# Batch 2's shifted copy of V moved from GpSimd's DMA queue to SyncE's, and batch 3's V preparation moved a few slots later

## The chip, the cores and the metric

The kernel runs on one core of a Trainium2 chip. Its time is the device time of one execution in microseconds (us); a figure for a kernel is the median of several executions. The engines of the core are called PE (TensorE: matrix products; PEld is its weight load), DVE (VectorE), ACT (ScalarE), POOL (GpSimd) and SP (SyncE, which here only issues DMAs). They run beside each other, each in its own order, and wait for one another by semaphores.

## The reference

Sliding-window causal attention (window 64, 8 batches, 8 heads, 576 positions, head size 64), then a layer norm and a two-layer MLP with a residual:

```python
scores = scale * np.matmul(q, k.transpose(0, 1, 3, 2))
mask = (rel >= 0) & (rel < window)          # rel = row position - column position, window = 64
scores = np.where(mask, scores, -1000000000.0)
attn = np.exp(scores - np.max(scores, axis=-1, keepdims=True))
attn = attn / (np.sum(attn, axis=-1, keepdims=True) + 1e-09)
x = np.matmul(attn, v)                      # then heads side by side: (8, 576, 512)
xn = (x - mu) / np.sqrt(var + 1e-06) * g_ln
out = x + np.maximum(xn @ w_ch1, 0.0) @ w_ch2   # 512 -> 2048 -> 512
```

## The kernel before

The first 512 rows of each batch are one group of 4 blocks of 128 rows; the last 64 rows of all 8 batches are a ninth group, "the tails". The main loop runs over groups g. PE's work in iteration g is the MLP of group g, written as a list of **units** (32 at g = 1: 16 units `l1_half` of 8 matmuls each, L586, and 16 units `l2` of 4 matmuls each, L456, four for each block). After unit i the kernel emits what was put into **slot** i with `at(i, function, arguments)`: the attention of batch g + 1 and the loads and casts of batch g + 2. There is no scheduler: within a slot, and so on each engine, the order of the `at` calls is the order of execution.

In iteration g = 1 the work around batch 2 and batch 3 is this.

- **V of batch 2.** `load_v` (L141) brings 512 rows of V in four 256 KB DMAs on SP's queue into `v32`, of which there is one buffer. `cast_v` (L147, POOL) casts it to fp16 into `vA`. The window of a block of 64 query rows reaches into the block of 64 keys before it, so a second copy `vB`, shifted by 64 rows, is made: `alloc_vB` (L151, POOL) clears the first 64 rows, and `make_vB` (L165 and L166) copies `vA` into `vB` with two DMAs from SBUF to SBUF, of 64 partitions each: 260 KB and 195 KB, issued on POOL's queue.
- **The product with V.** `b_pe` (L343, PE) multiplies the masked exponentials `pt` with `vA` and `vB`. Block 0 of batch 2 stands in slot 14, blocks 1, 2 and 3 in slots 17, 20 and 20. Block 0 needs the first of the two copies only. Its PSUM tile `xps` has one buffer, which held the scores of block 1 before; so it also needs ACT's second exponential of these (L309, slot 13).
- **Rows of x.** `b_rows` (L359 to L368, DVE) divides by the sums and takes mean and variance (`mvg`). `z_step` (L387 to L390, POOL) makes the normalized rows `z` of the block in four operations, and `zt_step` (L398) transposes them with a DMA on SP's queue into `zT`. The MLP of group 2 starts with `hps` (L444), whose first matmul needs all four transposes of batch 2. Its PSUM bank (two buffers) is that of block 2's `ch`, its second unit's that of block 3's; they are emptied by `add_out` (L466, DVE).
- **Batch 3.** SP issues its q and k in two halves (L94, slots 3 and 8), then its V (slot 10). POOL casts the first half of q and k in slot 8 (L128), the second in slot 14 behind block 0's `z_step`, and V, in two halves, in slot 18 (ahead of them the last element of each head's row is set to one, L135). `vB` of batch 3 is cleared and made in slot 20.

SP takes its instructions strictly in order, waits included.

Of the kernel before, what the change touches and what calls it, by code (L numbers as in the profile page):

```python
# [20 lines left out]
def kernel(  # L21
# [10 lines left out]
    nc = tc.nc  # L32
# [48 lines left out]
    qkT, vA, vB, pts = {}, {}, {}, {}  # L81
# [79 lines left out]
    def vB_prev(b, c, eng):  # L161
        evac(eng, vB[b][0:64, c + 1, :, 0:D], v32[b][64:128, c])

    def make_vB(b):
        nc.gpsimd.dma_start(out=vB[b][64:128, :], in_=vA[b][0:64, :])  # L165
        nc.gpsimd.dma_start(out=vB[b][0:64, 1:4], in_=vA[b][64:128, 0:3])  # L166

    wst = {}

# [619 lines left out]
    for i in range(8):  # L789
# [7 lines left out]
        out=mask[0:64], in_=mask[0:64], compare_op=ALU.is_gt, fill=0.0,  # L797
# [3 lines left out]
        out=mask[64:128], in_=mask[64:128], compare_op=ALU.is_ge, fill=0.0,  # L801
# [88 lines left out]
    for g in range(NGRP):  # L890
# [7 lines left out]
        def at(i, f, *a):  # L898
            slots[min(i, len(slots) - 1)].append((f, a))

        def first_scores(b, i):
            at(i, s_pe, b, 0)
            at(i, s_pe, b, 1, False, "xps")
            at(i, s_exp, b, 0, 0, 1)
            at(i + 1, s_exp, b, 1, 0, 1)
            at(i + 1, s_mask, b, 0)
            at(i + 2, s_mask, b, 1)

        b = g + 1
# [33 lines left out]
        if g == 1:  # L943
            at(0, cast_qk, 2, 0)
            at(0, cast_qk, 2, 1)
            at(0, b_step, 1, 2)
            at(2, b_step, 1, 3)
            at(4, zt_step, 1, 2)
            at(4, root, 1)
            at(6, zt_step, 1, 3)  # L950
            at(4, alloc_v, 2)
            at(4, alloc_qkT, 2)
            at(4, alloc_vB, 2)
            at(5, cast_v, 2, 0, 4)
            at(5, make_vB, 2)
            at(4, t_main, 2, 0, 0)
            at(5, t_main, 2, 1, 0)
            at(7, t_main, 2, 0, 1)
            at(7, t_main, 2, 1, 1)
            at(7, w2_sums, 3, 0, 4)  # L960
            at(8, w2_sums, 3, 4, 8)
            at(25, w2_sums, 2, 0, 4)
            at(28, w2_sums, 2, 4, 8)
            at(9, s_pe, 2, 0)
            at(9, s_pe, 2, 1, False, "xps")
            at(9, s_exp, 2, 0, 0, 1)
            at(10, s_mask, 2, 0)
            at(11, s_exp, 2, 1, 0)
            at(13, s_exp, 2, 1, 1)
            at(13, s_mask, 2, 1)  # L970
            for j in range(4):
                i = (14, 17, 20, 22)[j]
                if j < 3:
                    at(i, b_pe, 2, j)
                if j < 2:
                    at(i, s_mm, 2, j + 2)
                    at(i + 1, s_mask, 2, j + 2)
                if j == 2:
                    at(i, b_pe, 2, 3, "sc")
                at(i, b_rows, 2, j)  # L980
                at(i, z_step, 2, j)
                at((18, 21, 24, 27)[j], zt_step, 2, j)
            at(3, load_qk, 3, 0)
            at(8, load_qk, 3, 1)
            at(10, load_v, 3, 0, 4)
            at(8, alloc_qkT, 3)
            at(8, cast_qk, 3, 0)
            at(14, cast_qk, 3, 1)
            at(18, alloc_v, 3)
            at(18, cast_v, 3, 0, 2)  # L990
            at(18, cast_v, 3, 2, 4)
            at(20, alloc_vB, 3)
            at(20, make_vB, 3)
            first_scores(3, 30)
            for i, (x, half) in zip((12, 24, 18, 28), ((0, 0), (1, 0), (0, 1), (1, 1))):
                at(i, t_main, 3, x, half, 0)
            at(40, load_qk, 4, 0)
            at(40, load_qk, 4, 1)
            at(40, load_v, 4, 0, 2)
# [58 lines left out]
        if g > 1 and n < B:  # L1058
            at(3, load_v, n, 2, 4)
            at(17, alloc_v, n)  # L1060
            at(17, cast_v, n, 0, 2)
            at(17, cast_v, n, 2, 4)
            at(21, alloc_vB, n)
            at(21, make_vB, n)
            for i, (x, half) in zip((13, 18, 13, 22) if g == 2 else (13, 17, 13, 21),
                                    ((0, 0), (1, 0), (0, 1), (1, 1))):
                at(i, t_main, n, x, half, 0)
            first_scores(n, 27)
            if n + 1 < B:
                at(40, load_qk, n + 1, 0)  # L1070
                at(40, load_qk, n + 1, 1)
                at(40, load_v, n + 1, 0, 2)
# [61 lines left out]
```

## Time and profile before

| | us |
|---|---|
| median of three runs (308.37, 309.27, 311.14) | 309.27 |
| profiled execution | 308.48 |
| span from first to last instruction of the profiled execution | 306.6 |
| PE busy | 293.8 (96%) |
| DVE busy | 215.3 (70%) |
| POOL busy | 172.8 (56%) |
| ACT busy | 150.2 (49%) |
| mean granted clock of TensorE | 0.991 |

The profile's times count from the start of the span. A line of the timeline gives start, duration, engine, line, operation, output<-inputs, how many, and in brackets the idle time of the engine before it with the releaser. A line of the chain of waits gives start, duration and what ran. A line of a table by stages gives the stretch, its length, the busy time of each engine with the number of instructions, the granted clock (1.00 is full), the busy share of the DMA engines (above 1 where transfers overlap) and GB/s. "us to landing" runs from the start of a DMA's issue to its completion. A wait for several things is put down by the profile to the one that came last by its records.

### The profile page before, as it was taken

To read this page: it belongs to the slowest core of one execution; us is meant where nothing else is said; L and a number is where in the kernel's file an instruction comes from. 1 tells how busy PE (TensorE), PEld (TensorE's weight loads), DVE (VectorE), ACT (ScalarE), POOL (GpSimd) and SP (SyncE) were. 2 spreads that over 40 slices of the span, in tenths; PEclk is the share of its full clock that TensorE was granted. 3 is DMA by queue.
4 is the path that set the end of the run, shared out by engine and by line. 5 is a ranking of instruction groups with operands and counts; after the bars stand their busy time and mean duration, and the time that the engine had idled before them with its cause. 6 is when DMAs were issued, how large, how long until landed. Compare 5 with 4: busy or idle time off the path is not lost.

```text
span 306.6 us, 7574 instructions
## 1 busy us (share of the span) xinstructions
PE 293.8 (96%) x3061; PEld 196.7 (64%) x3061; DVE 215.3 (70%) x416; ACT 150.2 (49%) x253; POOL 172.8 (56%) x258
## 2 busy tenths in 40 slices
PE   6999999997998999999999999999999999999992
PEld 4557545785454459755965597559655854788882
DVE  0688695763573898469856874699568875789972
ACT  2496635686216753785247527852475046306500
POOL 7589676472791778378817964688128507014300
PEclk9999999999899999999999999999999999999998
DMA  8999999999756999799269997996619397003014
GB/s 192 265 385 303 314 362 270 282 262 244 156 125 188 285 188 162 219 321 181 41 206 319 191 195 214 318 136 97 214 31 181 69 188 190 19 17 139 0 37 103
DMA packets 113669, 58.35 MB, mean 190 GB/s; under 512 B 83617, under 2 KB 104609, under 8 KB 113634
## 3 DMA queue, kind: packets, MB, share of 16 engines
q1 hardware_dynamic: 112576, 54.67, 73.9%
q0 software_dynamic: 768, 2.80, 3.8%
q8 instruction: 24, 0.39, 0.6%
q10 hardware_dynamic: 290, 0.40, 0.5%
q14 instruction: 11, 0.09, 0.1%
HBM read 38.80 MB, written 9.44 MB: 157 GB/s over the span
## 4 chain that ended last, share of the span: by engine, by line
PE 85%; DMA 4%; ACT 3%; DVE 3%; SPq 3%; POOL 1%; issue 1%; POOLq 0%
PE hps L444 29%; PE pA L521 12%; PE pB L521 8%; PE pC L521 8%; PE ch L456 5%; PE xps L343 4%; PE sc L299 3%; PE hph L586 3%; SPq L141 3%; DMA vB<-vA 2%; PE ch L603 2%; PE tp L229 2%; PE lA L641 2%; PE warm L811 2%; DMA v<-in_v_dram 1%; PE lC L641 1%
## 5 line engine op out<-in xcount | busy, mean ns | idle before, releaser
L444 PE MATMUL hps<-zT,w1g 128*128 128x512 f16 x416 | 94.6, 379 | 0.9 <-DVE xn L466 0.9
L448 ACT ACTIVATE hrT<-hps 128x512 f16<-128x512 f32 x104 | 62.4, 600 | 42.1 <-PE hps L444 38.7
L444 PEld LDWEIGHTS <-w1g 128*128 128x128 f16 x416 | 39.2, 98 | 46.4 <-issue 3.4
L309 ACT ACTIVATE pt<-sc 128x512 f16<-128x512 f32 x72 | 39.3, 599 | 26.2 <-PE sc L299 25.6
L387 POOL TENSOR_SCALAR rsz<-mvg 128x1 f32<-128x1 f32 x28 | 10.9, 390 | 63.5 <-DVE mvg L368 62.5
L521 PEld LDWEIGHTS <-sS 128*128 128x128 f16 x448 | 43.3, 98 | 4.9
L128 POOL CAST qk<-qk 128x1024 f16<-128x1024 f32 x32 | 35.6, 1126 | 11.2 <-DMA qk<-in_k_dram 4.6
L316 DVE TENSOR_TENSOR pt<-pt,mask 128x1024 f16<-128x1024 f16 x32 | 25.3, 795 | 19.5 <-ACT pt L309 19.5
L521 PEld LDWEIGHTS <-hrT 128*128 128x128 f16 x336 | 32.1, 98 | 6.4 <-ACT hrT L448 1.0
L215 ACT COPY qkT<-tp 128x1024 f16<-128x1024 f16 x16 | 16.1, 1013 | 34.0 <-PE tp L229 24.2
L521 PE MATMUL pC<-w2s,sS 128*128 128x256 f16 x224 | 26.9, 273 | 0.0
L521 PE MATMUL pA<-wT,sS 128*128 128x256 f16 x224 | 26.9, 273 | 0.0
L363 DVE TENSOR_TENSOR xn<-xps,rcp 128x512 f32<-128x512 f32 (+1 forms) x47 | 25.6, 564 | 0.9
L365 DVE BATCH_NORM_STATS2 stats<-xn 128x6 f32<-128x512 f32 x36 | 25.0, 695 | 1.2
L495 DVE TENSOR_TENSOR sS<-hrT 128x512 f16<-128x512 f16 (+1 forms) x40 | 24.2, 606 | 2.2 <-ACT hrT L448 2.1
L586 PE MATMUL hph<-zT,w1g 128*128 128x256 f16 x192 | 23.7, 276 | 0.6 <-DVE zT L407 0.5
L390 POOL TENSOR_SCALAR z<-xn,rsz 128x512 f16<-128x512 f32 x28 | 21.9, 782 | 2.9
L359 DVE RECIPROCAL rcp<-xps 128x8 f32<-128x8 f32 (+1 forms) x47 | 7.7, 183 | 19.3 <-PE xps L343 19.3
L388 POOL TENSOR_TENSOR rsz<-rsz,mhalf 128x1 f32<-128x1 f32 x28 | 19.8, 706 | 2.3
L586 PEld LDWEIGHTS <-w1g 128*128 128x128 f16 x192 | 18.2, 99 | 3.4 <-DVE zT L407 0.7
L456 PE MATMUL ch<-w2s,hrT 128*128 128x512 f16 x80 | 20.0, 398 | 0.0
L343 PEld LDWEIGHTS <-pt 128*64 128x64 f16 x576 | 11.5, 110 | 12.6 <-issue 8.0
(116 smaller groups left out, 443.0 us busy)
## 6 DMA issues: line engine op xcount, KB each, us to landing
out_dram<-xn SPq DMA_DIRECT2D x33, 256.0 KB, 2.4
qk<-in_q_dram SPq DMA_DIRECT2D x16, 512.0 KB, 6.5
qk<-in_k_dram SPq DMA_DIRECT2D x16, 512.0 KB, 7.3
v<-in_v_dram SPq DMA_DIRECT2D x32, 256.0 KB, 7.5
w2s<-in_moe_w_ch_dram SPq DMA_DIRECT2D x9, 512.0 KB, 9.3
w1s<-in_moe_w_ch_dram SPq DMA_DIRECT2D x4, 512.0 KB, 6.6
tk<-in_k_dram SPq DMA_DIRECT2D x8, 256.0 KB, 4.7
tv<-in_v_dram SPq DMA_DIRECT2D x8, 256.0 KB, 5.0
```

Of the source, the lines that this page charges most:

```text
L128: nc.gpsimd.tensor_copy(out=dst[:, :].rearrange("p (a j) e d -> p a e j d", j=j), in_=t[:, :].rearrange("p (a e j d) -> p a e j d", e=2, j ...
L309: nc.scalar.activation(out=o, in_=i, func=AF.Exp, bias=0.0, scale=scale)
L316: nc.vector.tensor_tensor(out=ptv, in0=ptv, in1=mb, op=ALU.mult)
L343: nc.tensor.matmul(out=tiles[h // n][64 * r:64 * r + 64, h % n, :D + 1], lhsT=pt[:, par, hp, r, :], rhs=rhs, start=True, stop=True)
L363: nc.vector.tensor_tensor(out=xn[:, n * i:n * i + n], in0=xps[:, :, 0:D], in1=rcp_b, op=ALU.mult)
L365: nc.vector.bn_stats(out=stats, in_=xv)
L444: nc.tensor.matmul(out=hps, lhsT=w1g[:, kc, 128 * hc:128 * (hc + 1)], rhs=zT[g][:, kc, :], start=(kc == 0), stop=(kc == NKC - 1),)
L448: nc.scalar.activation(out=hrT[:, hc, :], in_=hps, func=AF.Relu, bias=0.0, scale=1.0)
L456: nc.tensor.matmul(out=ch[kb], lhsT=hrT[:, hc, 128 * kb:128 * (kb + 1)], rhs=w2s[:, hc, :], start=(hc == 0), stop=(hc == NHC - 1),)
L495: nc.vector.tensor_tensor(out=o, in0=x, in1=y, op=op)
L521: nc.tensor.matmul(out=o, lhsT=a[:, c, 128 * p:128 * p + 128], rhs=wv[:, c, :], start=(first and (p == 0 or split_c) and c == 0), stop=(c ...
L586: nc.tensor.matmul(out=hps[:, e], lhsT=w1g[:, kc, 128 * hc:128 * (hc + 1)], rhs=zT[g][:, kc, 256 * half:256 * half + 256], start=(kc == 0) ...
```

## The change

`make_vB` takes the issuing engine as an argument. Batch 2's copy (g = 1, slot 5) is issued on SP's queue; the one call of `make_vB` with another engine than POOL. On SP's queue slot 5 lies behind the first half of batch 3's q and k (slot 3) and ahead of the second (slot 8) and of batch 3's V (slot 10).

For batch 3 the second half of the V cast goes from slot 18 to 21, and `alloc_vB` and `make_vB` (still on POOL's queue) from slot 20 to 23. On POOL the order after block 1's `z_step` was: cast of both halves, `z_step` of block 2, clearing of `vB`, two DMA issues, `z_step` of block 3. It becomes: cast of the first half, `z_step` of block 2, cast of the second half, `z_step` of block 3, clearing of `vB`, two DMA issues. No other engine's order changes.

```diff
-    def make_vB(b):
-        nc.gpsimd.dma_start(out=vB[b][64:128, :], in_=vA[b][0:64, :])
-        nc.gpsimd.dma_start(out=vB[b][0:64, 1:4], in_=vA[b][64:128, 0:3])
+    def make_vB(b, eng=nc.gpsimd):
+        eng.dma_start(out=vB[b][64:128, :], in_=vA[b][0:64, :])
+        eng.dma_start(out=vB[b][0:64, 1:4], in_=vA[b][64:128, 0:3])
...
             at(5, cast_v, 2, 0, 4)
-            at(5, make_vB, 2)
+            at(5, make_vB, 2, nc.sync)
...
             at(18, cast_v, 3, 0, 2)
-            at(18, cast_v, 3, 2, 4)
-            at(20, alloc_vB, 3)
-            at(20, make_vB, 3)
+            at(21, cast_v, 3, 2, 4)
+            at(23, alloc_vB, 3)
+            at(23, make_vB, 3)
```

## The prediction

> **What bounds the kernel now.** PE is busy for 96% of the span, so a gain must close PE's idle time, give it a better clock, or leave it less to do. I first asked who PE waits for:
>
> ```profile
> PE xps L343 <- DMA vB<-vA: 2.2, 1, 2.2
> PE hps L444 <- DVE xn L466: 0.9, 1, 0.9
> ```
>
> Columns: total us, how often, longest. Apart from a 2.3 us start-up wait these are the two largest waits of PE, both inside iteration g = 1. The first is the transfer that the change moves. The chain of waits shows it in place:
>
> ```profile
> 64.87 1.90 POOL vA L147
> 66.77 0.29 issue
> 67.06 7.63 DMA vB<-vA
> 74.69 0.14 issue
> 74.83 0.45 PE xps L343 x16
> 75.28 0.34 PE sc L299 x16
> 75.62 1.48 PE hph L586 x8
> 77.09 2.91 PE ch L456 x8
> 80.00 0.38 PE xps L343 x16
> ```
>
> The copy of batch 2's V lands 7.63 us after POOL issued it, and block 0's product with V starts at 74.83. What follows is slow too: 8 hph matmuls in 1.48 us, 8 ch matmuls in 2.91. The table by stages says why (busy time of PE, PEld, DVE, ACT and POOL, then the granted clock, the DMA share and GB/s):
>
> ```profile
> 72.60:74.80 2.20, 0.00 (x1) 0.00 (x0) 0.69 (x1) 0.66 (x2) 0.00 (x0) 1.00 1.07 207
> 76.30:77.00 0.70, 0.70 (x5) 0.52 (x4) 0.68 (x1) 0.44 (x1) 0.00 (x0) 0.50 0.40 83
> 77.00:78.00 1.00, 1.00 (x4) 0.34 (x3) 0.76 (x2) 0.60 (x1) 0.54 (x2) 0.50 1.02 228
> 78.00:79.00 1.00, 1.00 (x3) 0.30 (x2) 0.00 (x0) 0.00 (x0) 0.79 (x3) 0.50 0.73 166
> ```
>
> After 2.2 us without a matmul the clock falls to half, to be back only at about 79.2. POOL's timeline and one line of SP's give the other wait its cause:
>
> ```profile
> 77.38 0.44 POOL L387 TENSOR_SCALAR rsz<-mvg 128x1 f32<-128x1 f32 x1 [5.35 <-DVE mvg L368]
> ...
> 79.66 2.02 POOL L128 CAST qk<-qk 128x1024 f16<-128x1024 f32 x2
> 82.40 0.53 POOL L387 TENSOR_SCALAR rsz<-mvg 128x1 f32<-128x1 f32 x1 [0.72 <-DVE mvg L368]
> ...
> 84.80 2.03 POOL L147 CAST vA<-v 128x1024 f16<-128x1024 f32 x2
> 86.92 0.19 POOL L387 TENSOR_SCALAR rsz<-mvg 128x1 f32<-128x1 f32 x1
> ...
> 91.03 0.18 POOL L387 TENSOR_SCALAR rsz<-mvg 128x1 f32<-128x1 f32 x1
> ...
> 92.33 0.76 POOL L390 TENSOR_SCALAR z<-xn,rsz 128x512 f16<-128x512 f32 x1
> ```
>
> ```profile
> 93.11 1.20 SPq L398 DMA_TRANSPOSE zT<-z x1
> ```
>
> PE stops at 95.24 and goes on at 96.10 with hps. The profile names the add L466 that ended at 96.04, but the first hps unit takes the bank of block 2's ch, emptied by 91.45; only the second needs the later one. It also needs all four transposes, and the last of them, of block 3's z (ended 93.09), took 2.7 us from 93.11. So POOL's z chain holds PE here, some 3.0 us from the end of z to the first matmul. From 96 to 301 us PE has no idle time worth naming: 204.86 us busy of 205.00. What g = 1 gains goes to the end.
>
> **Part 1, the copy on SP's queue.** POOL loses two DMA issues (0.75 + 0.53 us, 67.06 to 68.36); it idles 0.89 us right after, until q arrives, so that is worth nothing. SP gains two issues and a wait: the first must wait for the V cast, over at 66.77. Queued behind it are batch 3's second q/k half (issued at 64.05 and 64.60 before), its four V loads (from 66.79) and all transposes.
>
> The trace has no such copy on SP's queue. An SP issue costs 0.33 us (out store) to 1.10 us (the q load at 62.30). From issue to landing: at best 2.3 us (the out store of 256 KB at 96.06, in a quiet queue), at worst 10.6 us (a V load issued at 67.2). So the first copy lands between 66.8 + 2.3 = 69.1 and 77.4. I take about 71.5, because of one row: the q load issued at 64.05 took 8.4 us and landed at 72.45, right behind the k load issued at 63.50 (7.4 us, 70.9). The copy takes that q load's place behind the k load with half its bytes, and no second queue beside it.
>
> Then PE no longer waits for the copy. Next is ACT: block 0's tile is free only when the exponential at 72.18 ends (0.59 us), so it starts at 72.85 instead of 74.83: **1.98 us**. A wait of 0.25 us takes the place of 2.23.
>
> The clock: 8 hph and 8 ch matmuls took 75.62 to 80.00, 4.38 us. At full clock 8 hph take 0.88 (63.80 to 64.68) and 8 ch 1.75 (half of the 3.45 and 3.56 of 16): 2.63. **1.75 us**; the table gives the same: 2.7 us at 0.50, with 0.7 us at 0.75 ahead of them and 1 us at 0.82 behind, lose 1.35 + 0.18 + 0.18 = 1.7. In sum block 1's product starts at 76.3 instead of 80.00: 3.7 us ahead.
>
> The Trainium skill, "TensorE: Matmul & The Clock Gate", section "HAM oscillation", gives as its rule that PE gaps above some 3.4 us are the ones that cost the clock. By it this gap of 2.2 us would be free and the 1.75 us would drop out of the sum; the row shows half clock after it, and decides.
>
> The q/k half issued after the copies starts some 4 us later, at 68.0. Two loads at the distances seen (1.5 and 0.9 us) behind the copies land by about 75. POOL casts them once block 0's z is done, which after the change is 77.9: a cover of 3 us. The V loads start near 69 and land near 80 to 81, as before or 1 us later; the first two are wanted at 82.3, the last two at 86.
>
> **Part 2, and the end of the chain.** PE's ch ends at 95.25 - 3.71 = 91.54. Is z there? Block 0's rows now start behind the mask (72.81, 0.69 us) that stands ahead of them on DVE, so `mvg` comes 1.87 us after 73.5, and POOL starts z at 75.56. From there on POOL has work without a break, by the durations above: z of block 0 2.31 (77.38 to 79.69), two casts 2.02, z of block 1 2.40, the ones and half a V cast 1.1, z of block 2 2.48 (86.92 to 89.40), the other half 1.0, z of block 3 2.06, some 0.15 between. That is 13.5 us: z ends at 89.1 and hps starts 3.0 later, at **92.1**. Without part 2, clearing and issuing (89.35 to 91.03, 1.7 us) would stand ahead of z, and hps would start at 93.8. So PE waits 0.55 us where it waited 0.86, and iteration 2 starts at 92.1 instead of 96.10: **4.0 us** earlier. If it had been the add L466 after all, hps would start at 91.54 + 0.85 = 92.4; the sum hardly depends on it.
>
> Batch 3's `vB` is issued behind z: cleared by 89.6, landed 3.9 us (the 89.82 issue's time) later at 93.5. Its first reader stood 2.7 us behind hps, so at 94.8: 1.3 us to spare. If that cover goes, PE waits there.
>
> The sum: 1.98 + 1.75 + 0.86 - 0.55 = 4.0 us. The profiled execution took 308.48 (span 306.6), so 304.5. That execution lies 0.8 below the median of the three runs; I keep its own time as base, and the range has room for the rest.
>
> **The rivals.**
>
> *The copy comes late, but earlier than before.* The DMA engines were full from 67 to 75 us (busy share above 1), and an empty slot arises while SP waits for the cast. If it lands at 74.0, block 0 starts at 74.1, POOL's chain ends 1.25 us later (hps at 93.35), PE's own way at 92.8 with the full clock or 94.5 with the loss. 305.8 to 306.9. Against it: the 72.45 row.
>
> *It does not do what it says.* If the bytes ahead set the landing and not the queue, the copy lands at 74.7 as ever. Then part 2 alone acts: z is 1.7 us earlier, and the 0.86 us goes. 307.6.
>
> *The other side.* SP's queue is worse than POOL's for this copy: it waits behind everything SP has issued, and transfers issued on SP in those microseconds took 7.1 to 10.6 us. The product starts later than before from 8.0 us on (66.8 + 8.0 = 74.8), and the whole is slower from 8.9, when the 0.86 us is used up too. At 10.6 us block 0 starts at 77.5, 2.7 us late, with the clock lost as before; less the 0.86 us, 1.8 us slower: 310.3. Against it: those 8.4 to 10.6 us were spent behind 1 to 2 MB, of which only some half a megabyte would be left ahead of the copy.
>
> A rule speaks for this rival: "DMA: Bandwidth & Descriptors", section "Queues, rings and completion order", has each DMA engine take turns between queues packet by packet. On a queue of its own the copy should get its turn at once, and giving that up should cost. The measured 7.6 us for 260 KB, against 3.9 at 89.82 in a quieter stretch, shows little of such a privilege.
>
> **How the numbers follow.** Forecast, 303.4 to 305.5 (POOL's durations good to half a us, PE's own way alone giving 303.9): 0.67. Late copy, 305.8 to 306.9: 0.16. No effect of part 1, 307.6: 0.09. Slower, 310.3: 0.08. Predicted 304.5; leaving out the last case and most of what lies above, the range is 303.2 to 307.7. About 1% (3.1 us) is what a measurement of this kernel can tell from no change. Faster by over 1%, below 305.4: 0.66. Slower by over 1%, above 311.6, needs the last case and more: 0.04. Within: 0.30.
>
> **What would show it.** The wait of xps on vB gone from PE's list, block 0's product right behind the exponential of slot 13, half clock nowhere between 72 and 84 us; block 1's product near 76.3; POOL without a break from 75.6 to 89; hps starting 3 us after block 3's z, and half a microsecond of idle PE before it. It would be wrong if the copy took over 6 us, if batch 3's second q/k half landed after 77.9 (each microsecond later moves z and hps as much), or if batch 3's `vB` came after 94.8.

## The result and the profile after

The changed kernel takes 306.07 us (median of six, 305.05 to 307.14) where the kernel before took 310.14 in the same batches (six, 308.37 to 311.38): 4.1 us, a ratio of 0.987 with the 95% interval 0.983 to 0.991. A second measurement gave 0.988 (0.984 to 0.991). Ratios in this document leave disturbed executions out (those over 1.5% above the fastest of their kernel); medians and spreads count all. The profiled execution took 305.05 us, its span 303.2.

PE's waits from 90 us to the end of the span (after), ACT's second exponential of block 1's scores, and the start of block 0's product with V on PE's timeline:

```profile
PE hps L444 <- DMA zT<-z: 1.3, 1, 1.3
```

```profile
71.94 0.59 ACT L309 ACTIVATE pt<-sc 128x512 f16<-128x512 f32 x1
```

```profile
72.63 0.19 PE L343 MATMUL xps<-vB,pt 128*64 128x65 f16 x1 [0.27 <-issue]
...
76.06 0.22 PE L343 MATMUL xps<-vB,pt 128*64 128x65 f16 x1
...
92.64 2.79 PE L444 MATMUL hps<-zT,w1g 128*128 128x512 f16 x12 [1.28 <-DMA zT<-z]
```

The 2.2 us wait for vB is gone, 0.27 us is left; the profile names no releaser for it ("issue"), but ACT's exponential ended at 72.53, 0.1 us before the product, while the copy had landed at 71.4. Block 1's product follows 3.43 us later, where it took 5.17. The wait before hps is now put down to the transpose itself, and has grown from 0.86 to 1.28 us. SP's timeline, and the landing time of its first copy:

```profile
61.70 0.38 SPq L94 DMA_DIRECT2D qk<-in_q_dram  x1
62.17 0.59 SPq L94 DMA_DIRECT2D qk<-in_k_dram  x1
68.08 0.56 SPq L165 DMA_DIRECT2D vB<-vA  x1
68.68 0.58 SPq L166 DMA_DIRECT2D vB<-vA  x1
69.32 0.60 SPq L94 DMA_DIRECT2D qk<-in_q_dram  x1
69.96 0.86 SPq L94 DMA_DIRECT2D qk<-in_k_dram  x1
70.86 6.56 SPq L141 DMA_DIRECT2D v<-in_v_dram  x4
```

```profile
vB<-vA SPq DMA_DIRECT2D x1, 260.0 KB, 3.3
```

SP stands still from 62.8 to 68.08, until POOL has cast batch 2's V (1.3 us later in this execution than in the profile before), and then the copy lands in 3.3 us, at 71.4. The table by stages (busy PE, PEld, DVE, ACT, POOL, then granted clock, DMA share, GB/s) has full clock where it was half:

```profile
72.60:74.80 2.20, 2.17 (x43) 1.75 (x44) 2.13 (x4) 1.77 (x4) 0.00 (x0) 1.00 0.99 301
...
77.00:78.00 1.00, 1.00 (x6) 0.49 (x5) 0.97 (x2) 0.97 (x2) 1.00 (x2) 1.00 1.20 221
78.00:79.00 1.00, 1.00 (x7) 0.44 (x5) 0.97 (x4) 0.00 (x0) 1.00 (x2) 1.00 1.02 208
```

And POOL's chain, from block 0's z to block 3's:

```profile
75.22 0.46 POOL L387 TENSOR_SCALAR rsz<-mvg 128x1 f32<-128x1 f32 x1 [4.29 <-DVE mvg L368]
...
77.49 2.48 POOL L128 CAST qk<-qk 128x1024 f16<-128x1024 f32 x2
...
85.75 1.04 POOL L147 CAST vA<-v 128x1024 f16<-128x1024 f32 x1
...
88.41 0.76 POOL L390 TENSOR_SCALAR z<-xn,rsz 128x512 f16<-128x512 f32 x1
89.11 0.52 POOL L151 MEMSET vB<- 64x520 f16 x1
89.58 0.75 POOL L165 DMA_DIRECT2D vB<-vA  x1
```

No bracket but the first: POOL has no idle time between 75.2 and 90.9.

### The profile page after: what moved, and what is told of

The parts are those of the page before. It is cut to its first block, busy times and chain, and to the rows that moved or that the text cites. A ratio compares the mean times of both kernels' runs of the same rounds, so it can differ in the third digit from the quotient of the medians.

```text
span 303.2 us, 7570 instructions
## 1 busy us (share of the span) xinstructions
PE 291.2 (96%) x3061; PEld 195.4 (64%) x3061; DVE 217.5 (72%) x416; ACT 150.1 (49%) x253; POOL 172.1 (57%) x256
## 4 chain that ended last, share of the span: by engine, by line
PE 80%; POOL 5%; SPq 4%; DVE 3%; DMA 3%; issue 1%; ACT 1%; POOLq 0%
PE hps L444 30%; PE pA L521 12%; PE pB L521 8%; PE pC L521 8%; PE hph L586 6%; PE xps L343 3%; PE ch L603 3%; PE sc L299 2%; PE lA L641 2%; PE tp L229 2%; DMA w1s<-in_moe_w_ch_dram 2%; SPq L141 2%; POOL w1g L190 1%; DVE vB L217 1%; SPq L89 1%; PE lC L641 1%
## 5 line engine op out<-in xcount | busy, mean ns | idle before, releaser
L128 POOL CAST qk<-qk 128x1024 f16<-128x1024 f32 x32 | 36.4, 1150 | 9.3 <-DMA qk<-in_q_dram 4.6
L147 POOL CAST vA<-v 128x1024 f16<-128x1024 f32 (+2 forms) x19 | 17.5, 936 | 3.6 <-DMA v<-in_v_dram 3.6
L456 PE MATMUL ch<-w2s,hrT 128*128 128x512 f16 x80 | 18.8, 380 | 0.0
```

What stands on the lines that cost most here:

```text
L128: nc.gpsimd.tensor_copy(out=dst[:, :].rearrange("p (a j) e d -> p a e j d", j=j), in_=t[:, :].rearrange("p (a e j d) -> p a e j d", e=2, j ...
```

## The experiments

The theory at the start was that both waits of PE in g = 1 are for transfers (vB of batch 2, the last transpose), that part 1, the copy on SP's queue, removes the first with the clock's loss behind it, and that part 2, batch 3's V work in later slots, keeps POOL's chain short enough for the second. The rivals were that part 1 alone is the gain, that SP's queue as such is faster, and that the clock alone pays.

### Each part alone

Part 1 alone (`p1_alone`) leaves out this half of the change:

```diff
-            at(21, cast_v, 3, 2, 4)
-            at(23, alloc_vB, 3)
-            at(23, make_vB, 3)
+            at(18, cast_v, 3, 2, 4)
+            at(20, alloc_vB, 3)
+            at(20, make_vB, 3)
```

> Only the copy of batch 2's V goes to SP's queue; batch 3's V cast, clearing and copy stay in slots 18 and 20. Theory (the sum of the prediction): PE's wait for vB is gone and the clock stays full, but clearing and two DMA issues (1.7 us) stand ahead of block 3's z again, so PE waits some 2.5 to 3 us for the last transpose ahead of hps. Hps starts some 1.7 us later than in the changed kernel; 2.0 to 2.5 us faster than before. Rival (part 1 is the whole gain, hps is held by the add L466 and not by z): as fast as the changed kernel, 4 us faster than before.

Measured: 307.64 us (ten, 306.48 to 308.29) against 308.36 before, ratio 0.9975 (0.9951 to 0.9998): some 0.8 us. PE's wait from 90 us on, and the start of hps:

```profile
PE hps L444 <- DMA zT<-z: 2.3, 1, 2.3
```

```profile
73.17 0.19 PE L343 MATMUL xps<-vB,pt 128*64 128x65 f16 x1 [0.27 <-issue]
94.20 2.79 PE L444 MATMUL hps<-zT,w1g 128*128 128x512 f16 x12 [2.30 <-DMA zT<-z]
```

The mechanism is the expected one: no wait for vB, but a longer one for z, since clearing and issuing stand ahead of block 3's again. Hps starts 21.0 us after block 0's product, in the changed kernel 20.0 (92.64 - 72.63). The rival falls. The delay is 1.0 and not 1.7 us: block 3's z ends 1.5 us later after block 0's product than in the changed kernel, but its transpose lands in 2.85 us instead of 3.3. Yet the gain is smaller than the 2.0 to 2.5 us. The profiled execution (306.65) is 1.7 us below the median of the kernel before; four of the ten, at a mean clock of 0.989 to 0.993, took 307.7 to 308.3, the others 306.5 to 308.2. A gap of 2.3 us now stands ahead of hps, as long as the one that was followed by half clock before. In the profiled execution no half clock follows it. The slower executions have no profile, so that the clock took the rest there is an argument, not shown.

Part 2 alone (`p2_alone`) puts batch 2's copy back on POOL's queue:

```diff
-            at(5, make_vB, 2, nc.sync)
+            at(5, make_vB, 2)
```

> Only batch 3's V work moves; batch 2's copy stays on POOL's queue in slot 5. Theory: the wait for vB (some 2.2 us) and the half clock behind it stay; block 3's z ends 1.7 us earlier and hps follows ch without a gap: 0.9 us faster than before. Rival (the add L466 holds hps): the gap of 0.9 us stays, no gain.

Measured: 308.87 us (ten, 307.04 to 311.88) against 308.36, ratio 1.001 (0.998 to 1.005). A miss: no gain. PE's waits in its profiled execution (307.90):

```profile
PE xps L343 <- DMA vB<-vA: 1.8, 1, 1.8
PE hps L444 <- DVE pt L316: 1.6, 1, 1.6
PE hps L444 <- DMA zT<-z: 0.7, 1, 0.7
```

The wait for vB stayed, but here the clock held, and PE reached hps earlier than z: a gap of 1.6 us (the chain of POOL, z ending at 90.8 and the transpose 3.5 us later; the mask that the profile names ended within 0.2 us of it). A further 0.7 us is lost some iterations later, behind a transpose of z that took 6.0 us.

So in the medians the parts are not additive: 0.8 us and nothing alone, 3 to 4 together (3.9 to 4.1 for the changed kernel in its two batches; in this batch a kernel as fast as it, `v_cast_last` below, gained 3.3). In the profiled executions they nearly are, as far as the start of hps: 96.10 before, 94.20 with part 1, 94.58 with part 2, 92.64 with both, which is 1.9 and 1.5 us alone and 3.5 together. What the other executions with one part alone lose is not shown. Either part alone leaves PE a gap of about 2 us (2.3 and 1.8), the changed kernel none over 1.3 there; half clock behind such a gap, in some executions, would account for a part of it.

### Is it the queue, or what stands ahead in it?

`sp_behind_qk`, the copy on SP's queue but behind batch 3's second half of q and k:

```diff
-            at(5, make_vB, 2, nc.sync)
+            at(9, make_vB, 2, nc.sync)
```

> The changed kernel with batch 2's copy on SP's queue behind the second half of batch 3's q and k instead of ahead of it. Theory (what counts is how many bytes stand ahead of the copy in the queue): it lands 1 MB or some 3 us later than in the changed kernel, at 74 to 75 us; PE waits 1.5 to 2.5 us again, with half clock behind it; most of the gain is lost, 0 to 1.5 us faster than before. Rival (SP's queue serves the copy faster than POOL's, wherever it stands): landing 3 to 4 us after the issue as in the changed kernel, and its time.

Measured: ratio 0.997 (0.994 to 1.001), median 308.99, ten executions from 306.05 to 314.74, the four slowest at a mean clock of 0.984 to 0.987. In the chain of waits:

```profile
67.51 7.25 DMA vB<-vA
...
74.89 0.46 PE xps L343 x15
```

The copy takes 7.25 us instead of 3.3, on the same queue and issued within 0.6 us of the same time, and PE waits 2.05 us for it; most of the gain is lost. So SP's queue as such gives nothing. The half clock that was expected behind the wait is not in the profiled execution.

`pool_held` is the other way round: the copy on POOL's queue, the second half of q and k kept back behind the first V load, which waits for the same V cast:

```diff
-            at(5, make_vB, 2, nc.sync)
+            at(5, make_vB, 2)
-            at(8, load_qk, 3, 1)
-            at(10, load_v, 3, 0, 4)
+            at(10, load_v, 3, 0, 1)
+            at(10, load_qk, 3, 1)
+            at(10, load_v, 3, 1, 4)
```

> The changed kernel with batch 2's copy back on POOL's queue, but the second half of batch 3's q and k issued on SP behind the first of batch 3's V loads, which itself waits for batch 2's V cast: the copy has about as little ahead of it in the DMA engines as in the changed kernel, on the other queue. Theory (bytes ahead count, not the queue): the copy lands 3.5 to 4.5 us after its issue, PE does not wait for it, and the time is within 1 us of the changed kernel's. Rival (POOL's queue is the slow one): 6.9 to 7.6 us, and the wait of 2 us is back, as in the kernel with batch 3's V work moved alone.

Measured: 306.48 (ten, 305.62 to 307.88) against 309.01, ratio 0.991 (0.989 to 0.994). Two DMAs of it:

```profile
vB<-vA POOLq DMA_DIRECT2D x1, 260.0 KB, 6.0
qk<-in_k_dram SPq DMA_DIRECT2D x1, 512.0 KB, 8.8
```

PE waits 1.3 us. Neither side was right: the copy, issued at 67.70, 0.14 us ahead of the q load, lands in 6.0 us: not the 3.3 us of the same order on one queue, and less than the 6.9 to 7.6 us with 1 MB issued earlier. It is not a pure test of the queue: a V load of 256 KB was issued 0.28 us ahead of the copy, which the changed kernel does not have there, and there the q load follows the copy only after 1.24 us.

`act_queue`, the copy on ACT's queue, SP's loads as before the change:

```diff
-            at(5, make_vB, 2, nc.sync)
+            at(8, make_vB, 2, nc.scalar)
```

> The changed kernel with batch 2's copy on ACT's queue (slot 8) and SP's loads as before the change, so the second half of batch 3's q and k stands ahead of the copy in time, but on another queue. Theory (the DMA engines serve the queues in shares, and 1.5 MB of SP's loads are ahead or beside): landing 6 to 7.6 us after the issue, PE waits some 2 us, as in the kernel with batch 3's V work moved alone. Rival (a hardware queue of its own gets its turn at once): landing 3 to 4 us after the issue, no wait for vB, and the time of the changed kernel, apart from what ACT loses by waiting for the V cast in slot 8 (below 1 us).

Measured: 307.95 (ten, 306.54 to 311.82) against 309.01, ratio 0.998 (0.994 to 1.002).

```profile
vB<-vA ACTq DMA_DIRECT2D x1, 260.0 KB, 7.3
```

```profile
PE xps L343 <- DMA vB<-vA: 1.3, 1, 1.3
PE hps L444 <- DMA zT<-z: 1.3, 1, 1.3
PE hph L586 <- ACT hrT L591: 0.9, 2, 0.5
```

A second hardware queue beside SP's gives 7.3 us, as POOL's did. In sum: beside or behind SP's 1 MB of q and k, on any of the three queues, the copy took 6.9 to 7.6 us (five profiles); on POOL's queue with the megabyte issued at the same time 6.0 (one profile); ahead of it on the same queue 3.3 to 3.4 in six profiles of seven, and 5.1 in the seventh, where the k load ahead of it had landed late too (8.8 us after its issue, in the others where it is recorded 5.9 to 7.2). What the change buys is a place ahead of the megabyte in SP's queue. Whether the one queue does it, or the 1.2 us by which the loads are then issued behind the copy, `pool_held` does not separate.

### What the half clock is worth

`p2_fill` is part 2 alone with ten unused matmuls where PE waits for vB:

```diff
+        def fill(n):
+            f = ps_t.tile([128, 512], FP32, tag="t1", name="fill")
...
+                nc.tensor.matmul(out=f[:, :].rearrange("p (a i) -> p a i", i=64), lhsT=ident16, rhs=mb,
+                                 start=True, stop=True)
...
+            at(14, fill, 10)
             for j in range(4):
```

> The kernel with batch 3's V work moved alone, and 10 idle matmuls of 512 columns (2.2 us at full clock, into an unused PSUM bank) put on PE ahead of block 0's product with vB, where PE waits for the copy: the wait stays, PE is busy in it. Theory (the half clock follows from the gap; but POOL's chain from block 0's z on sets the start of hps, so the clock is worth little of its own): granted clock 1.00 throughout, hps starts 19.5 to 20.3 us after block 0's product, 0 to 0.6 us faster than without the filling. Rival (the clock's loss goes straight to the end): 1.7 us faster than without it. Rival (the half clock does not come from the gap): half clock between 74 and 82 us as before.

Measured: 308.39 (ten, 307.73 to 308.99) against 309.01, ratio 0.999 (0.997 to 1.001). The clock is 1.00 in every stretch from 70 to 82 us, and the mean clock of all ten executions is 0.995 or more. So the half clock comes from the gap. Hps starts at 95.07, 20.4 us after block 0's product at 74.66, where 19.5 to 20.3 were expected: POOL's chain holds it. The ratio is 0.0024 below that of part 2 alone, but that lies within both intervals, and only two of the ten executions of part 2 alone had a mean clock below 0.99; so this pair does not price the clock.

The executions of the kernel before price it better. Of the 25 beside `p1_alone`, 14 with a mean clock of at most 0.991 had a median of 308.66, the 11 others 308.09; of the 25 beside `p2_fill`, 18 with at most 0.992 had 309.1, the 7 others 308.7. That is 0.4 to 0.6 us, where the direct effect on PE is 1.75. The profile before shows a way for it: POOL idles 0.72 us ahead of block 1's z (the line at 82.40 in the prediction), since block 1's rows come late; no profile with full clock there has this gap. The rest of the loss runs beside POOL's chain, which would have kept PE waiting anyway.

### What holds the changed kernel now

`v_cast_last` takes the second half of the V cast out of POOL's chain:

```diff
-            at(21, cast_v, 3, 2, 4)
+            at(23, cast_v, 3, 2, 4)
```

> The changed kernel with the second half of batch 3's V cast (1.0 us on POOL) moved from slot 21 to 23, behind block 3's z. Theory (POOL's chain from block 0's z to block 3's z now sets the start of hps): z of block 3 ends 1.0 us earlier, PE's wait for the transpose falls from 1.3 us to about 0.3, 1.0 us faster than the changed kernel and about 5 us faster than before; batch 3's vB lands when it did. Rival (the add L466, or the landing of the transpose whenever it is issued, is the bound): no gain over the changed kernel.

Measured: 305.07 (four) against 308.36, ratio 0.989 (0.986 to 0.992). Hps follows ch without a gap, 18.6 us after block 0's product instead of 20.0, so z and its transpose were the bound. Two things moved here: z of block 3 ends 1.2 us earlier after block 0's product, and its transpose lands in 2.4 us instead of 3.3, since batch 3's copy is now issued 1.8 us behind it and not 0.4. But the time did not fall by as much as expected. PE's only wait from 90 us on (times in the whole span: 123.37):

```profile
PE hps L444 <- DMA zT<-z: 0.6, 1, 0.6
```

It stands one iteration later. For a measure on one chip it ran again beside the changed kernel:

> The changed kernel itself, as the measure for the other kernels of this batch on the same chip. Expected 1.0 to 1.6% faster than before, as in its first measurement (ratio 0.987).

> The kernel with the second half of batch 3's V cast behind block 3's z, once more, beside the changed kernel. Theory (what hps of iteration 2 gains is partly given back one iteration later, where the transpose of batch 3's block 2 landed 5.6 us after its issue): 0.3 to 0.8 us faster than the changed kernel. Rival (the later landing was chance): 1.0 us faster.

Measured: the changed kernel 305.60 (ratio 0.988, 0.984 to 0.991), this one 305.40 (0.987, 0.983 to 0.990). Its chain shows the gain given back again; the line below is from the changed kernel:

```profile
117.53 0.54 POOL vB L165
...
118.34 5.43 DMA zT<-z
...
123.81 0.39 PE hps L444
```

```profile
118.49 0.59 POOL L165 DMA_DIRECT2D vB<-vA  x1
```

The transpose of batch 3's block 2 takes 5.4 us, against 2.5 to 3.3 for the two of that stretch in the changed kernel, and PE stands still for 1.2 us at 123.8. It happened in both profiled executions, and in both batch 4's copy of V had been issued just ahead of the transpose, 0.1 and 0.9 us, on POOL's queue; in the changed kernel the copy (118.49) came 0.7 us behind the transpose (117.8). In all thirteen profiles the six transposes of z issued less than 1 us behind such a copy took 4.5 to 5.6 us, those issued 0.4 to 0.6 us ahead of one, where the landing is recorded, 3.3 to 4.3. It fits that POOL, done earlier, brings the copy in front of the transpose, but no run tested this by itself.

`vb3_sp` changes the other term, the transpose's landing, by moving batch 3's copy behind it:

```diff
-            at(23, make_vB, 3)
+            at(28, make_vB, 3, nc.sync)
```

> The changed kernel with batch 3's copy of V too on SP's queue, behind the transpose of block 3's z (slot 28). Theory (the transpose lands 3.3 instead of 2.4 to 2.7 us after its issue because batch 3's copy, issued 0.4 us later on POOL's queue, takes DMA time from it): landing 2.4 to 2.7 us, hps 0.6 to 0.9 us earlier, 0.6 to 0.9 us faster than the changed kernel. Rival (the landing has nothing to do with that copy): as the changed kernel.

Measured: 305.00 (six, 304.44 to 305.38), ratio 0.985 (0.982 to 0.989), 0.6 us faster than the changed kernel beside it; the intervals overlap. The landing of the last transpose, in the changed kernel and in this one:

```profile
zT<-z SPq DMA_TRANSPOSE x1, 3.3
```

```profile
zT<-z SPq DMA_TRANSPOSE x1, 2.4
```

PE's wait falls from 1.3 to 0.4 us, hps starts 19.1 us after block 0's product. The theory holds for the mechanism: the copy that part 2 moved behind z ran beside the last transpose and cost it 0.9 us. The other profiles agree: this transpose took 3.3 to 3.6 us in the seven that issue the copy 0.4 us behind it, 2.4 in the four that issue it later.

Both edits together (`both`):

> The edits of the two kernels before it together: batch 3's second V cast behind block 3's z, and batch 3's copy on SP's queue behind the last transpose. Theory: PE has no wait between ch and hps; 1.2 us faster than the changed kernel, the fastest of all, if the copy lands ahead of its reader (some 3 us after hps starts); copy issued at about 90.5, landing by 94. Rival: the copy, now behind the cast and on SP ahead of batch 4's loads, comes late and PE waits for it: slower than the changed kernel.

Measured: 305.13 (six, 304.55 to 307.01), ratio 0.987 (0.984 to 0.991): no better than either. In the profiled execution batch 2's V came later (copy issued at 69.79 instead of 66.8 to 68.1), so that PE waited 0.8 us for vB, a wait of the changed kernel's own part 1, and 0.5 for the transpose. So there is no version clearly faster than the changed kernel; `vb3_sp` has the lowest median.

## Why the prediction was right

It said 304.5 us from a profiled base of 308.48, 4.0 us faster, and 4.1 were measured. That the two agree to 0.1 us is luck: in the two profiled executions, which the sum is about, the gain is 3.4 us, and the forecast of 304.5 itself lies 1.6 below the measured median, since the base lay 1.7 below the median of the kernel before (310.14). In the terms of the sum, 1.98 + 1.75 + 0.86 - 0.55, the profiles have 2.20 + 1.74 + 0.86 - 1.28 = 3.5. Step by step:

- **The copy** was to land at 71.5: it landed at 71.4. Here two errors cancel: it was issued 1.3 us later than taken (68.08 for 66.8), and took 3.3 us where 4.7 were taken from the q load's row; in `vb3_sp`, issued at 66.79, it landed at 70.1. `sp_behind_qk` shows that the reason given was right: the place ahead of the megabyte, and not SP's queue as such.
- **Block 0's product**, 72.85 forecast, 72.63 measured, 0.1 us behind ACT's exponential as forecast. **Block 1's**, 76.3 and 76.06.
- **The clock**: no half clock left, as forecast. But the 1.75 us is a figure of one execution and of PE's own way; executions of the kernel before with and without a low clock differ by 0.4 to 0.6 us. It did no harm in the sum, because the sum's last term, PE's new wait, was taken from the end of POOL's chain.
- **POOL without a break**: 75.56 to 89.1 forecast, 75.22 to 89.17 measured. The chain took 0.4 us longer than its sum of 13.5, since the two casts of q and k took 2.48 us for 2.02.
- **Hps**, 92.1 forecast, 92.64 measured. The term that was mis-sized is the way from block 3's z to the first matmul: 3.0 us forecast, 3.5 measured, since the transpose landed in 3.3 us instead of 2.7. The step counted what part 2 takes away ahead of z, and batch 3's copy only as a deadline (93.5 forecast, 89.58 + 3.7 = 93.3 measured); it did not count that copy as a neighbour of the last transpose. `vb3_sp` showed it.
- **Without part 2** hps was to start 1.7 us later: 1.0 measured (`p1_alone`), in good part by the same mis-sized term; the median lost more than that besides.
- **The covers** held: q and k of batch 3 landed at 74.6 and 76.1, wanted at 77.5.

The profile before had a row for the term that was mis-sized. Block 2's transpose there, with batch 3's copy issued 0.4 us behind it, took 3.5 us, where block 0's took 2.4 (block 1's took 3.5 too, but its issue alone took 1.9 us instead of 1.2):

```profile
89.43 1.19 SPq L398 DMA_TRANSPOSE zT<-z  x1
```

```profile
89.82 0.59 POOL L165 DMA_DIRECT2D vB<-vA  x1
```

```profile
zT<-z SPq DMA_TRANSPOSE x1, 3.5
```

Of the rivals, a late copy is what `sp_behind_qk`, `pool_held` and `act_queue` made; the changed kernel never showed it in a profile. The other side's mechanism, a wait behind what SP has issued, is real as soon as the megabyte stands ahead, but then SP's queue is as slow as POOL's (7.25 us and 6.9 to 7.6), not worse. Nor did a queue of its own help the copy: 7.3 us on ACT's.

The rule of 3.4 us from the Trainium skill ("TensorE: Matmul & The Clock Gate", section "HAM oscillation") did not fit: a gap of 2.2 us was followed by half clock in the profile before. Nor does the length of the gap alone decide in these profiles: gaps of 1.8 (`p2_alone`), 2.05 (`sp_behind_qk`) and 2.3 us (`p1_alone`) were not followed by it. The same page of the Trainium skill, section "What's actually happening", has the window that watches PE run free of the kernel; this would explain why half clock strikes some executions only, which no run here shows.

## What to carry to other kernels

When a wait for a small transfer is the bound, look at what the DMA engines are doing for later work: issued ahead of them on the same queue, the small transfer came first here (3.3 us); on another queue it took 6.0 to 7.6 us. After removing a wait of PE, follow the engine that feeds the next one to its last instruction and its last DMA, including the DMAs that the change places next to it; here the copy that part 2 put behind z cost the last transpose 0.9 us. And time two edits together as well as alone: here 0.8 us and nothing in the medians alone, 3 to 4 together. And price a lower clock only on the path that ends last.

## What the runs showed of the hardware

- A 260 KB copy inside SBUF, issued right behind the cast of its data, took 3.3 us (once 5.1) ahead of 1 MB of loads on its queue, 7.25 behind them on it, 7.3 beside them on ACT's, 6.9 to 7.6 on POOL's, 6.0 on POOL's with the loads issued at the same time.
- Half clock after a gap of about 2 us does not come in every execution: the profiled execution with it had a mean clock of 0.991, and 14 of 25 executions of the kernel before had at most 0.991, 18 of 25 at most 0.992 in another batch. With ten unused matmuls in the gap the mean clock was 0.995 or more in ten of ten.
- A DMA transpose of 128 x 512 fp16 landed in 2.4 us when little ran beside it, in 3.3 to 3.6 (the last one of batch 2) with two copies of together 455 KB issued 0.4 us later, and in 4.5 to 5.6 when such copies were issued less than 1 us ahead of it.
